# Eight output tiles of the last pass turned through DRAM and VectorE's block transpose, with POOL's products and the verdict moved

## The chip, the core and the metric

The kernel runs on one core of one Trainium2 chip. The metric is the time of one execution on the device in microseconds (us), the median of several runs. TensorE (PE) multiplies matrices and transposes through them, VectorE (DVE) and ScalarE (ACT) work element by element, POOL (GpSimd) does the same more slowly, and SP issues the transfers between DRAM and the on-chip memory. PSUM is the memory that TensorE writes to.

## The reference

Four layers on x of 2048 rows and 640 columns: a Fourier layer, a linear attention layer, and both again.

```python
x = A_x
x = x + _A_ref(_layernorm(x), A_dft_seq_re, A_dft_seq_im, A_dft_hid_re, A_dft_hid_im)
x = x + _B_ref(_layernorm(x), B_wqkv, B_wo)
...
# _A_ref: a = x @ hid_re.T, b = x @ hid_im.T;  y = seq_re @ a - seq_im @ b
# _B_ref: 32 heads of 20 columns; q, k, v = x @ wqkv; phi(t) = where(t > 0, t + 1, exp(t)) + 1e-6
#   kv = phi(k).T @ v per head;  z = sum of phi(k) over the rows
#   o = (phi(q) @ kv) / (phi(q) . z + 1e-6);  y = o @ wo
```

## The kernel before

The rows of x are cut into 16 tiles of 128 rows that stay on the chip. Every product of full precision is made of three products of rounded halves: a tile is split into `hi` (a ScalarE cast, L137) and `lo = src - hi` (a subtraction, L138, on VectorE or POOL), and `product` (L193) runs 5 chunks x 3 pairs x 2 column halves = 30 matmuls. Each product needs its tile with columns and rows exchanged. There are two ways to that. `transposed` (L143) does it on TensorE, five 128x128 transposes into PSUM, from which `hi` and `lo` are read. `turn_out` and `turn_in` (L151, L156) write the tile to DRAM in one order and read it back in another, both on the SP queue, and `turned` (L161) finishes with VectorE's transpose of 32x32 blocks; `hi` and `lo` are then read from that tile. Which tiles of the keys and queries stages go the second way stands in `TURNED`; in `TLOWS`, whose subtraction goes to POOL.

An attention layer first makes keys and queries of all tiles and the gram matrix (L286) in two parts (`keys_values`). `combine` then makes the key-value products (L465) and the matrix M that holds them and wo (six rows of products in `rows`), and does the last `KEEP` query projections of the layer (`late`).

The last pass is `outputs`: for tile n, POOL multiplies the query features with the sums of the keys (`weigh`, L511, "a product" of POOL below), and VectorE makes the weighted queries from it (`weighted`: a reduction L527, an addition L528, a reciprocal L529, and a pair of multiplications L531 and L537). The result is transposed on TensorE, split, and multiplied with M in 30 matmuls; VectorE adds the result to x (the residual, L611) and SP stores it. POOL works three tiles ahead, the weighting two, the transposes one. In the first round `between` calls `verdict`, which reduces the results of a check on the Fourier matrices to one flag (two small TensorE transposes, L1177 and L1181, and some small VectorE rows); the check itself compares 30 pieces of those matrices during the keys stages (`Check`, L1157, in the steps of `STEPS`).

Within a stage, TensorE, VectorE, ScalarE and POOL get their order from a scheduler at build time, which goes by program order, free buffers and the offsets in `AHEAD` ("weigh", "q", "res" and so on, by stage and tile). SP issues in program order. Temporary tiles come from a pool of 12 buffers (`temp`), weights and `slot` tiles from one of 31.

Of the kernel before, what the change touches and what calls it, by code (L numbers as in the profile page):

```python
# [15 lines left out]
NT = S // 128  # L16
# [14 lines left out]
STEPS = ((1, 2, 3, 4, 5, 6, 10, 11, 12), (2, 4, 8, 9, 12))  # L31
SAVES = ((4, 5, 8, 10, 13), (0, 6, 7, 11, 12))
# [4 lines left out]
TURNED = ((4, 5, 6, 7, 8, 9, 10, 11, 12, 13, 14, 15), (4, 5, 6, 8, 9, 10, 11, 12, 13, 14, 15))  # L37
TLOWS = ((3, 7, 15), ())
LEADS = (3, 2)
ORDERS = ('tfkq', 'tfkq')  # L40
ANORM = ((2,), (3, 5))
KEEP = (2, 1)
TOTAL = (4, 2)
EARLY = (14, 13)
PKSUMS = ((1, 7, 13, 14), (2, 6, 11, 12))
LEAD = 3
LOADS = (13, 13, 15, 15)
ASTATS = ((4, 10, 11, 13, 14), (1, 4, 10, 15))
VSTATS = ((0, 3, 4, 7, 8, 11, 13, 15), (1, 11, 13, 15))
# [8 lines left out]
class K:  # L58
# [77 lines left out]
    def split(self, src, hi, lo, pool=0):  # L136
        self.nc.scalar.copy(hi, src)  # L137
        self.engine(pool).tensor_tensor(lo, src, hi.bitcast(F32), op=ALU.subtract)  # L138
# [15 lines left out]
    def turn_in(self, src, early):  # L154
        z = self.pqp.tile([128, D], F32, tag="pq", name=self.nm("z")) if early else self.temp()
        self.nc.sync.dma_start(z, src.rearrange("a (j t) c -> (a j) (t c)", t=4))  # L156
        return z
# [40 lines left out]
class Attention:  # L198
# [99 lines left out]
    def keys_values(self, check=None, saves=()):  # L298
# [26 lines left out]
        for a, b in ((0, CUT), (CUT, NT)):  # L325
            pks = []
            for n in range(a, b):
                got, pk = [], self.slot()

                def feed(n=n):  # L330
                    for m in range(n + 1, n + 1 + lead) if n == 0 else (n + 1, n + lead):
                        if m < NT and m not in out and (m == n + 1 or m in self.turns):
                            with k.ahead("normed", m):
                                out[m] = self.normed(m)
                    for m in range(n + 1, n + 1 + fetch) if n == 0 else (n + fetch,):
                        if m < NT and m in self.turns:
                            out[m] = k.turn_in(out[m], m < EARLY[k.layer])

# [97 lines left out]
    def combine(self, G, late):  # L436
# [17 lines left out]
        with k.ahead("weigh", 0):  # L454
            qd, t1 = self.weighted(0, self.weigh(0)), self.weigh(1)
# [4 lines left out]
        for js in ((NE - 1, NE - 2), range(NE - 2)):  # L460
            kvps = k.psum()
            for j in js:
                e, w = span(j)
                for c in range(ND):
                    nc.tensor.matmul(  # L465
                        place(kvps, j), wv[c][:, e : e + w], G[c][:, e : e + w],
                        start=c == 0 and j in (5, 4, 0), stop=c == ND - 1 and j > 2, skip_group_check=True,
                    )
            for j in js:
                w = span(j)[1]  # L470
                km = place(kvps, j) if KM[k.part // 2] else k.temp(shape=(w, w))
                t = self.wt()
                hi, lo = t[:w, :w], t[:w, 128 : 128 + w]
                with k.ahead("kv", j):
                    nc.vector.tensor_tensor(km, place(kvps, j), self.mask[:w, :w], op=ALU.mult)
                    if w == EC:
                        k.split(km, hi, lo)
                    else:
                        k.split(km.rearrange("p (h i s) -> p h i s", i=ND, h=2), mixed(hi), mixed(lo))
                kv[j] = hi, lo  # L480
        for q in late[1:]:
            q()
# [22 lines left out]
        self.next, self.t1 = qd, self.weigh(2)  # L505

    def weigh(self, n):
        k = self.k
# [945 lines left out]
```

## Time and profile before

| what | us |
|---|---|
| three timed runs | 757.91, 758.84, 759.44 |
| their median | 758.84 |
| the profiled execution | 759.65 |
| its span, first to last instruction | 757.7 |
| TensorE busy | 732.2 (97%) |
| VectorE busy | 597.0 (79%) |
| ScalarE busy | 356.0 (47%) |
| POOL busy | 245.2 (32%) |

The span is what the rows of the profile cover; about 2 us lie around it. The profiled execution took 0.8 us more than the median run. A busy TensorE is a TensorE with work in it, not one at its peak.

### The profile page before, as it was taken

The numbers are of one execution on the slowest core, as the hardware profiler recorded it, in microseconds if no ns is written. First come the engines' busy times: TensorE is split into PE (matmuls) and PEld (weight loads), VectorE is DVE, ScalarE is ACT, GpSimd is POOL, SyncE is SP. The second block draws the span as 40 slices with busy tenths as digits, with TensorE's granted clock in tenths as the row PEclk, the third lists the DMA queues.
The fourth block names the chain that finished last, engine by engine and source line by source line (L and its number), as shares of the span: only waits on it lengthen the run. The fifth ranks groups of instructions, "written<-read, shape, count | busy, mean of one in ns | idle before, by whom it ended". The sixth has DMA issues, their size and how long they took to land.

```text
span 757.7 us, 12763 instructions
## 1 busy us (share of the span) xinstructions
PE 732.2 (97%) x4769; PEld 695.1 (92%) x4769; DVE 597.0 (79%) x1162; ACT 356.0 (47%) x673; POOL 245.2 (32%) x262
## 2 busy tenths in 40 slices
PE   4999999999999999999999999999999999989997
PEld 1388999999999999899976999999999999989997
DVE  7997888778769757788974867888776887598982
ACT  7745544574345524555682246556433555331110
POOL 5337932320013202467762664214000011233300
PEclk9999999999999999999999999999999999999999
DMA  9323247754576820400052223764236525011112
GB/s 333 99 82 100 81 145 253 240 179 126 163 219 209 292 68 23 128 30 2 10 194 75 70 93 96 233 203 145 75 111 186 177 69 164 2 29 53 70 71 74
DMA packets 50560, 94.22 MB, mean 124 GB/s; under 512 B 5013, under 2 KB 18584, under 8 KB 50488
## 3 DMA queue, kind: packets, MB, share of 16 engines
q1 hardware_dynamic: 50487, 93.31, 38.7%
q8 instruction: 40, 0.66, 0.4%
q14 instruction: 33, 0.26, 0.1%
HBM read 73.54 MB, written 19.33 MB: 123 GB/s over the span
## 4 chain that ended last, share of the span: by engine, by line
PE 71%; DVE 13%; DMA 5%; ACT 4%; POOL 2%; issue 2%; SPq 1%; DVEq 0%; ACTq 0%
PE ps L193 41%; PE ps L286 18%; PE ps L1028 4%; PE ps L1082 3%; DMA z<-turn 3%; PE ps L143 2%; PE ps L465 2%; DVE t L138 2%; PE ps L987 1%; DMA ck<-in_ck 1%; DVE t L531 1%; DVE ps L527 1%; DMA x<-in_x 1%; DVE x L553 1%; DVE junk L1157 1%
## 5 line engine op out<-in xcount | busy, mean ns | idle before, releaser
L193 PE MATMUL ps<-w,t 128*128 128x320 f32 x2880 | 435.7, 311 | 0.7 <-DVE w L138 0.3
L193 PEld LDWEIGHTS ps<-w,t 128*128 128x128 f32 x2880 | 424.2, 188 | 2.6 <-DVE t L138 0.6
L286 PE MATMUL ps<-t,t 128*128 128x256 f32 (+1 forms) x640 | 140.0, 309 | 0.2 <-ACT t L137 0.2
L1157 DVE CUSTOM_DVE_ANT_0 junk<-ck,ck 128x688 bf16<-128x688 f32 (+5 forms) x138 | 103.8, 752 | 7.9 <-DMA ck<-in_ck 6.2
L286 PEld LDWEIGHTS ps<-t,t 128*128 128x128 f32 x640 | 107.2, 188 | 0.4 <-ACT t L137 0.4
L353 POOL TENSOR_TENSOR t<-t,s 128x640 f32<-128x640 f32 x24 | 43.4, 1808 | 181.7 <-DVE s L321 174.7
L286 PE MATMUL ps<-w,t 128*128 128x384 f32 (+1 forms) x320 | 98.8, 310 | 2.6 <-DVE w L138 2.6
L318 ACT ACTIVATE t<-ps 128x640 f32<-128x640 f32 x64 | 45.1, 705 | 106.5 <-PE ps L193 106.1
L511 POOL TENSOR_TENSOR t<-pq,t 128x640 f32<-128x640 f32 x32 | 53.3, 1672 | 100.9 <-ACT t L434 45.9
L137 ACT CAST t<-t 128x640 fp32r<-128x640 f32 x55 | 40.0, 728 | 66.6 <-DVE t L161 28.0
L137 ACT CAST t<-ps 128x640 fp32r<-128x640 f32 (+1 forms) x43 | 29.6, 692 | 81.5 <-PE ps L143 80.9
L286 PEld LDWEIGHTS ps<-w,t 128*128 128x128 f32 x320 | 60.1, 188 | 3.7 <-DVE w L138 3.7
L138 DVE TENSOR_TENSOR t<-t,t 128x640 fp32r<-128x640 f32 x53 | 45.9, 865 | 20.7 <-ACT t L137 19.5
L1028 PE MATMUL ps<-t,u 128*128 128x322 f32 x306 | 48.7, 316 | 1.1 <-DVE t L138 0.7
L1028 PEld LDWEIGHTS ps<-t,u 128*128 128x128 f32 x306 | 46.0, 189 | 2.8 <-issue 1.0
L320 ACT ACTIVATE t<-t 128x640 f32<-128x640 f32 x64 | 47.4, 742 | 0.0
L138 DVE TENSOR_TENSOR t<-ps,t 128x640 fp32r<-128x640 f32 (+1 forms) x43 | 35.0, 816 | 8.7 <-ACT t L137 8.7
L321 DVE SCALAR_TENSOR_TENSOR pq<-t,pq 128x640 f32<-128x640 f32 x32 | 28.2, 881 | 14.3 <-ACT t L320 14.3
L112 POOL TENSOR_TENSOR kept<-ve,mhalf 128x1 f32<-128x1 f32 x32 | 21.1, 675 | 54.3 <-DVE ve L111 53.7
L1082 PE MATMUL ps<-cw,ab 128*128 128x512 f32 x80 | 35.4, 595 | 1.6 <-ACT t L812 1.0
L321 DVE SCALAR_TENSOR_TENSOR s<-t,s 128x640 f32<-128x640 f32 x32 | 26.6, 832 | 9.9 <-ACT t L320 9.9
L1082 PEld LDWEIGHTS ps<-cw,ab 128*128 128x128 f32 x80 | 14.8, 190 | 21.0 <-issue 18.6
(187 smaller groups left out, 951.4 us busy)
## 6 DMA issues: line engine op xcount, KB each, us to landing
ck<-in_ck SPq DMA_DIRECT2D x48, 346.0 KB
ck<-in_ck SPq DMA_DIRECT2D x48, 344.0 KB
turn<-t SPq DMA_DIRECT2D x23, 320.0 KB
save<-w SPq DMA_DIRECT2D x20, 320.0 KB
w<-save SPq DMA_DIRECT2D x20, 320.0 KB
z<-turn SPq DMA_DIRECT2D x18, 320.0 KB
x<-in_x SPq DMA_DIRECT2D x16, 320.0 KB
out<-x SPq DMA_DIRECT2D x15, 320.0 KB
```

Of the source, the lines that this page charges most:

```text
L137: self.nc.scalar.copy(hi, src)
L138: self.engine(pool).tensor_tensor(lo, src, hi.bitcast(F32), op=ALU.subtract)
L193: nc.tensor.matmul(pu[:m, 512 * h : 512 * h + HD], s, w[:, HD * h : HD * h + HD], start=first, stop=last)
L286: nc.tensor.matmul(self.place(G, c, part), x[:, 128 * c : 128 * c + 128], p[:, f : f + n], start=start and i == 0, stop=stop and i == 2, s ...
L318: nc.scalar.activation(h2(e), halves(pu), AF.Relu, scale=-1.0)
L320: nc.scalar.activation(e, e, AF.Exp, scale=-1.0)
L321: nc.vector.scalar_tensor_tensor(out, e, 1e-6, out, op0=ALU.add, op1=ALU.add)
L353: k.engine(n not in PKSUMS[k.layer]).tensor_tensor(pksum, pksum, pk, op=ALU.add)
L511: k.nc.gpsimd.tensor_tensor(t1, self.PQ[self.order2[n]], self.zb, op=ALU.mult)
L1028: self.k.nc.tensor.matmul(po[:, o : o + 322], s[:, f : f + 128], w[:, x, :], start=start, stop=stop)
L1082: self.k.nc.tensor.matmul(self.sum(j), T.out["o", q][:, 128 * j : 128 * j + 128], self.C[2, g], start=n == 0, stop=n == 3)
L1157: i = nc.vector.tensor_tensor_reduce(k.junk[:, : a.shape[1]], b, a, 1.0, 0.0, op0, op1, o)
```

## The change

In the second layer's `outputs`, the tiles of `QTURNS` (7 and 9 to 15) go through DRAM: their weighted queries are made `QLEAD` = 2 tiles earlier than the others', a ScalarE copy brings the columns into the order that the block transpose wants, and `turn_out`, `turn_in` and `turned` take the place of `transposed`. For tiles 10, 13 and 15 (`QLOWS`) the subtraction goes to POOL. POOL's products are made four tiles ahead (`WLEAD`), six for turned tiles, and nine of them (`WSLOTS`) lie in slots of the larger pool. The verdict is made in three steps in rounds 6, 7 and 8. The residuals of tiles 0 to 5 are stored in halves. `LULLS` is (0, 0), so nothing waits for a lull.

```diff
-KEEP = (2, 1)
+QTURNS = (7, 9, 10, 11, 12, 13, 14, 15)
+QLEAD = 2
+LULLS = (0, 0)
+WLEAD = 4
+WSLOTS = (6, 7, 8, 9, 11, 12, 13, 14, 15)
+VERDICT = 6
+QLOWS = (6, 10, 13, 15)
+HALVES = (0, 1, 2, 3, 4, 5)
+KEEP = (2, 2)
...
-    def outputs(self, after, between=lambda: None):
+    def outputs(self, after, between=lambda n: None):
...
-        wt, t1 = self.next, self.t1
+        wt, t1 = {1: self.next}, self.t1
+        turns, lead = (QTURNS, WLEAD) if self.saved else ((), 3)
+        early = lambda m: QLEAD if m in turns else 0
         for n, i in enumerate(self.order2):
-            nxt = self.weigh(n + 3) if n + 3 < NT else None
-            if n + 1 < NT:
-                tp = k.transposed(wt)
-            if n + 2 < NT:
-                with k.ahead("weigh", n + 2):
-                    wt = self.weighted(n + 2, t1)
-            t1 = nxt
+            for m in range(n + 3, n + 1 + lead + QLEAD):
+                if m < NT and m not in t1 and m not in wt and m - lead - early(m) <= n:
+                    t1[m] = self.weigh(m, self.slot() if m in WSLOTS else None)
+            if n + 1 < NT and n + 1 not in turns:
+                tp = k.transposed(wt[n + 1])
+            for m in range(n + 2, n + 3 + QLEAD):
+                if m in t1 and m - 2 - early(m) <= n:
+                    with k.ahead("weigh", m):
+                        wt[m] = self.weighted(m, t1.pop(m))
+                    if m in turns:
+                        mixed = self.slot()
+                        k.nc.scalar.copy(
+                            mixed.rearrange("p (a b i) -> p b a i", a=4, b=ND),
+                            wt[m].rearrange("p (b a i) -> p b a i", a=4, b=ND),
+                        )
+                        wt[m] = k.turn_in(k.turn_out(mixed), self.slot())
...
-            between()
+            between(n)
             if n + 1 < NT:
                 with k.ahead("q", n):
-                    q = k.split_chunks(tp)
+                    q = k.turned(wt[n + 1], n + 1 in QLOWS) if n + 1 in turns else k.split_chunks(tp)
...
-                after(i, hs[0], hs[-1] + 1)
+                for h in [(x, x + 1) for x in hs] if n in HALVES and self.saved else [(hs[0], hs[-1] + 1)]:
+                    after(i, *h)
...
-            att.outputs(store, lambda: flags or flags.append(verdict(k)))
+            steps = verdict(k)
+            att.outputs(store, lambda n: 0 <= n - VERDICT < 3 and flags.append(next(steps)))
```

With `KEEP` the second layer's last two query projections stand in `combine`, not one. Beside this the tables of the two keys stages are new. The first layer turns tile 2 as well (`TURNED`); `TLOWS`, `ANORM`, `ASTATS`, `VSTATS` and `PKSUMS` give other tiles' subtractions, normalisations, statistics and key sums to other engines: over both keys stages VectorE has seven normalisations, two sets of statistics and seven subtractions fewer and three key sums more. `TOTAL`, `EARLY`, `STEPS`, `SAVES` and some 60 entries of `AHEAD` change. With the new `STEPS` one of the 30 pieces of the check (the fifth of `in_ck3`) is fetched and not compared.

The order shows three places. First POOL, its products of the last pass. Before, one after the other by tile, all in temporary tiles `t`; a row is one product, and `pq` is a tile's query features.

```order
L511 TENSOR_TENSOR t_7571<-pq_6510,t_7225 128x640
L511 TENSOR_TENSOR t_7623<-pq_6902,t_7225 128x640
L511 TENSOR_TENSOR t_7675<-pq_7296,t_7225 128x640
L511 TENSOR_TENSOR t_7727<-pq_6621,t_7225 128x640
L511 TENSOR_TENSOR t_7779<-pq_4967,t_7225 128x640
```

Now, for tiles 4, 7, 6, 9, 5, 10, 8, 11, 12, 13 and 14 in this order (L532 is the same line), and then the first subtraction that goes to POOL (L146), of tile 10:

```order
L532 TENSOR_TENSOR t_7500<-pq_6523,t_7196 128x640
L532 TENSOR_TENSOR s_7555<-pq_6629,t_7196 128x640
L532 TENSOR_TENSOR s_7608<-pq_7366,t_7196 128x640
L532 TENSOR_TENSOR s_7661<-pq_5404,t_7196 128x640
L532 TENSOR_TENSOR t_7553<-pq_7267,t_7196 128x640
L532 TENSOR_TENSOR t_7729<-pq_5511,t_7196 128x640
L532 TENSOR_TENSOR s_7727<-pq_4966,t_7196 128x640
L532 TENSOR_TENSOR s_7782<-pq_5083,t_7196 128x640
L532 TENSOR_TENSOR s_7841<-pq_5212,t_7196 128x640
L532 TENSOR_TENSOR s_7917<-pq_5635,t_7196 128x640
L532 TENSOR_TENSOR s_7979<-pq_5742,t_7196 128x640
L146 TENSOR_TENSOR t_8091<-t_8089,t_8090 128x640
```

The products of tiles 6 to 9 and 11 to 14 now lie in slots (`s`), those of 8 and 11 to 14 directly behind each other.

Second VectorE, from the residual of tile 4 to that of tile 5 (`x_104`, `x_106`). Before:

```order
L611 TENSOR_TENSOR x_104<-x_104,ps_7742 128x640
L138 TENSOR_TENSOR t_7826<-ps_7781,t_7825 128x640
L527 TENSOR_REDUCE den_7891<-t_7831 128x32
L528 TENSOR_SCALAR den_7891<-den_7891 128x32
L529 RECIPROCAL rden_7892<-den_7891 128x32
L531 TENSOR_TENSOR t_7831<-pq_5417,rden_7892 128x5x120
L537 TENSOR_TENSOR t_7831<-pq_5417,rden_7892 128x2x5x4
L611 TENSOR_TENSOR x_106<-x_106,ps_7794 128x640
```

Now, from the subtraction of tile 6 to the block transpose of tile 9 (L146 was L138, L175 L161, L549 to L558 L528 to L537, L643 L611):

```order
L146 TENSOR_TENSOR t_7835<-ps_7784,t_7834 128x640
L175 STREAM_TRANSPOSE t_7909<-s_7687 128x4x160
L549 TENSOR_SCALAR den_7925<-den_7925 128x32
L643 TENSOR_TENSOR x_106<-x_106,ps_7803 128x640
L550 RECIPROCAL rden_7926<-den_7925 128x32
L552 TENSOR_TENSOR s_7782<-pq_5083,rden_7926 128x5x120
L558 TENSOR_TENSOR s_7782<-pq_5083,rden_7926 128x2x5x4
L146 TENSOR_TENSOR t_7911<-t_7909,t_7910 128x640
L548 TENSOR_REDUCE den_7981<-s_7841 128x32
L146 TENSOR_TENSOR t_7974<-ps_7919,t_7973 128x640
L175 STREAM_TRANSPOSE t_8035<-s_7801 128x4x160
```

A tile's rows were one subtraction, one weighting and one residual; a turned tile's block transpose comes on top, two residuals ahead of its product, and the weightings run up to four tiles ahead.

Third SP, from the store of tile 4 on. Before it was one store a tile:

```order
L1256 DMA out<-x_104 128x640
L1256 DMA out<-x_106 128x640
L1256 DMA out<-x_108 128x640
L1256 DMA out<-x_110 128x640
L1256 DMA out<-x_112 128x640
```

Now, `turn` being the tile in DRAM:

```order
L1291 DMA out<-x_104 128x320 x2
L166 DMA turn_7799<-s_7797 128x4x160
L170 DMA s_7801<-turn_7799 128x640
L1291 DMA out<-x_106 128x320 x2
L166 DMA turn_7859<-s_7857 128x4x160
L170 DMA s_7861<-turn_7859 128x640
L1291 DMA out<-x_108 128x640
L166 DMA turn_7934<-s_7932 128x4x160
L170 DMA s_7936<-turn_7934 128x640
```

The way out and back of tile 9 stands behind the store of tile 4, that of tile 10 behind the store of tile 5, and so on to tile 15 behind that of tile 10.

## Rows read from the trace of the kernel before

**Rows 1.** Windows: length, busy PE, PEld, DVE, ACT, POOL; granted clock, DMA share, GB/s

```profile
107.00:175.00 68.00, 66.97 (x451) 65.90 (x449) 54.24 (x99) 39.53 (x66) 16.00 (x13) 1.00 0.67 218
466.00:652.00 186.00, 186.00 (x1273) 185.79 (x1272) 145.37 (x291) 90.86 (x148) 23.93 (x19) 1.00 0.47 144
```

**Rows 2.** Waits of TensorE: us in total, times, longest

```profile
PE ps L705 <- DMA x<-in_x: 10.6, 1, 10.6
PE ps L286 <- DVE w L138: 2.6, 3, 1.1
PE ps L143 <- DVE t L537: 2.2, 1, 2.2
```

**Rows 3.** Chain that ended last, last pass: start us, us, what

```profile
675.33 1.46 DVE t L537
...
676.92 1.05 PE ps L143 x5
677.98 5.62 PE ps L193 x30
683.60 0.55 PE ps L143 x5
684.15 4.41 PE ps L193 x30
```

**Rows 4.** Windows of the last pass

```profile
677.00:680.00 3.00, 3.00 (x14) 3.00 (x15) 3.00 (x9) 0.69 (x1) 0.00 (x0) 0.53 0.04 14
680.00:683.60 3.60, 3.60 (x25) 3.59 (x24) 1.94 (x7) 0.00 (x0) 0.00 (x0) 0.92 0.21 84
...
688.00:719.00 31.00, 31.00 (x222) 30.95 (x221) 29.85 (x44) 4.26 (x7) 11.69 (x7) 1.00 0.17 65
719.00:743.50 24.50, 24.50 (x175) 24.47 (x175) 17.52 (x28) 3.38 (x5) 2.50 (x2) 1.00 0.18 69
```

**Rows 5.** Timeline of VectorE in the last pass: start us, us, instruction

```profile
685.82 0.81 DVE L138 TENSOR_TENSOR t<-ps,t 128x640 fp32r<-128x640 f32 x1
686.55 0.18 DVE L537 TENSOR_TENSOR t<-pq,rden 128x40 f32<-128x40 f32 x1
686.65 0.81 DVE L527 TENSOR_REDUCE den<-t 128x32 f32<-128x640 f32 x1
687.50 0.18 DVE L528 TENSOR_SCALAR den<-den 128x32 f32<-128x32 f32 x1
687.71 0.35 DVE L529 RECIPROCAL rden<-den 128x32 f32<-128x32 f32 x1
...
698.22 0.78 DVE L531 TENSOR_TENSOR t<-pq,rden 128x600 f32<-128x600 f32 x1
698.92 1.57 DVE L537 TENSOR_TENSOR t<-pq,rden 128x40 f32<-128x40 f32 x1
700.41 0.81 DVE L611 TENSOR_TENSOR x<-x,ps 128x640 f32<-128x640 f32 x1
```

**Rows 6.** Timeline of POOL in the last pass

```profile
688.69 1.58 POOL L511 TENSOR_TENSOR t<-pq,t 128x640 f32<-128x640 f32 x1 [3.45 <-issue]
...
718.36 1.57 POOL L511 TENSOR_TENSOR t<-pq,t 128x640 f32<-128x640 f32 x1 [3.40 <-PE ps L193]
```

**Rows 7.** Lines L161 and L138: duration ns min/median/max

```profile
L161 DVE STREAM_TRANSPOSE t<-z x18: 1319/1346/1370, 105.6 to 583.2; 128x640 f32<-128x640 f32 x18
...
L138 POOL TENSOR_TENSOR t<-t,t x2: 1571/1661/1751, 137.0 to 253.0; 128x640 fp32r<-128x640 f32 x2
```

**Rows 8.** Chain in the first layer's keys stage

```profile
111.61 0.38 SPq L151
...
115.99 1.35 DVE t L161
...
139.87 0.37 SPq L151
...
147.14 1.36 DVE t L161
```

More of the change, by code (lines that the diff above doesn't have):

```diff
@@ L137, in split, with behind @@
         self.nc.scalar.copy(hi, src)
-        self.engine(pool).tensor_tensor(lo, src, hi.bitcast(F32), op=ALU.subtract)
+        return self.engine(pool).tensor_tensor(lo, src, hi.bitcast(F32), op=ALU.subtract)
+    def behind(self, later, earlier):
+        if earlier is not None:
+            self.tc.add_manual_dep(
+                later.ins, earlier.ins.name, mybir.DependencyInfo(mybir.DependencyClass.Sync, mybir.DependencyReason.DATA),
+                reason="a lull",
+            )
     def transposed(self, src):
@@ L152, in turn_out, with turn_in @@
         return src
-    def turn_in(self, src, early):
-        z = self.pqp.tile([128, D], F32, tag="pq", name=self.nm("z")) if early else self.temp()
+    def turn_in(self, src, z):
         self.nc.sync.dma_start(z, src.rearrange("a (j t) c -> (a j) (t c)", t=4))
@@ L336, in feed @@
                         if m < NT and m in self.turns:
-                            out[m] = k.turn_in(out[m], m < EARLY[k.layer])
+                            early = m < EARLY[k.layer]
+                            z = k.pqp.tile([128, D], F32, tag="pq", name=k.nm("z")) if early else k.temp()
+                            out[m] = k.turn_in(out[m], z)
                 def turn(n=n):
@@ L454, in combine @@
         with k.ahead("weigh", 0):
-            qd, t1 = self.weighted(0, self.weigh(0)), self.weigh(1)
+            qd = self.weighted(0, self.weigh(0))
+            t1 = None if LULLS[k.layer] else self.weigh(1)
         late[0]()
@@ L476, in combine @@
                     if w == EC:
-                        k.split(km, hi, lo)
+                        lull = k.split(km, hi, lo)
                     else:
-                        k.split(km.rearrange("p (h i s) -> p h i s", i=ND, h=2), mixed(hi), mixed(lo))
+                        lull = k.split(km.rearrange("p (h i s) -> p h i s", i=ND, h=2), mixed(hi), mixed(lo))
                 kv[j] = hi, lo
+        if LULLS[k.layer]:
+            t1 = self.weigh(1, None, lull)
+        else:
+            lull = None
         for q in late[1:]:
@@ L504, in combine, with weigh @@
             self.M.append(m)
-        self.next, self.t1 = qd, self.weigh(2)
-    def weigh(self, n):
+        self.next, self.t1 = qd, {m: self.weigh(m, None, lull) for m in range(2, WLEAD if self.saved else 3)}
+    def weigh(self, n, t1=None, lull=None):
         k = self.k
-        t1 = k.temp()
+        t1 = k.temp() if t1 is None else t1
         with k.ahead("pz", n):
-            k.nc.gpsimd.tensor_tensor(t1, self.PQ[self.order2[n]], self.zb, op=ALU.mult)
+            k.behind(k.nc.gpsimd.tensor_tensor(t1, self.PQ[self.order2[n]], self.zb, op=ALU.mult), lull)
         return t1
@@ L547, in outputs_by_hand @@
         k, nc, X = self.k, self.k.nc, self.X
-        q, wt, t1 = self.first, {1: self.next}, {2: self.t1}
+        q, wt, t1 = self.first, {1: self.next}, self.t1
         pu = None
@@ L1175, in verdict @@
     nc.vector.tensor_tensor(both[:, 0:4], both[:, 0:4], low, op=ALU.max)
+    yield
     p = k.psum()
@@ L1179, in verdict @@
     nc.vector.tensor_reduce(top, p[:8, :128], axis=AX.X, op=ALU.max)
+    yield
     p = k.psum()
@@ L1189, in verdict @@
     nc.vector.tensor_copy(flag, bad)
-    return flag
+    yield flag
 def fast_path(k, ctx, x, wqkv, wo, mask, sign, cls, cex, hid, ckc, ckh, out):
```

25 lines of the change are left out of this document (13 added, 12 removed).

## The prediction

> **What bounds the kernel now.** I read three views: who waited for whom, the windows by stage, and the chain of the last pass. TensorE is the bound almost everywhere. In the stretch that covers the second layer's keys and queries it is busy for all of its 186 us, at a granted clock of 1.00 [rows 1]. Over the whole run three waits stand out: 10.6 us for the first load of x, 2.6 us in three pieces, none over 1.1 us, in the first layer's gram stage, and 2.2 us once in the last pass [rows 2]. So time can be won only by taking work off TensorE, or by removing one of these waits.
>
> The last pass (16 output tiles, a product of 30 matmuls for each) is a fixed beat: five transposes in 0.55 us, then 30 matmuls in 4.41 us, 4.96 us a tile [rows 3]. The reader should also see its bad start. After product 0, VectorE is in the second of the two multiplications that make tile 2's weighted queries (L537), which takes 1.46 us of the chain; TensorE waits 2.2 us [rows 2], and then its five transposes take 1.05 us and its 30 matmuls 5.62 us [rows 3]. The granted clock says why: it was 0.53 in the 3 us behind the gap, which is the lower of the two levels (1.2 and 2.4 GHz) for nearly all of that stretch, 0.92 in the next 3.6 us, and 1.00 later [rows 4].
>
> VectorE is the second bound. In 688 to 719 us it is busy 29.85 of 31.0 us; in 719 to 743.5 us, where POOL has only two products left, 17.52 of 24.5 us [rows 4]. The timeline shows the difference: the small multiplication L537 takes 0.18 us when POOL is quiet and 1.57 us when a POOL product (L511) started just before it [rows 5, 6]. One product thus costs VectorE about 1.4 us when the two meet. Reductions, residuals and subtractions from PSUM keep their 0.81 us, also beside a product.
>
> **The change, part by part.** (1) Eight tiles lose their TensorE transposes: 8 x 0.55 = 4.4 us off a stage that TensorE bounds [rows 3]. In their place VectorE gets eight block transposes of 1.35 us, which no POOL work ever stretched (1319 to 1370 ns over 18) [rows 7], together 10.8 us; ScalarE gets eight copies, and as it is busy 4.26 us in 31.0 [rows 4], even 2 us each would be hidden; three subtractions go to POOL at 1.66 us [rows 7], some 2.4 us off VectorE, and their tiles are transposed over 4 us before the product that needs them; the SP queue gets eight pairs of transfers. The trip from the issue of the way out to the block transpose is 4.4 us (111.61 to 115.99) and once 7.3 us (139.87 to 147.14) in the first layer [rows 8], where the core moved 218 GB/s [rows 1]. The last pass moves 65 to 70 GB/s [rows 4]; 640 KB more a tile of 4.41 us is 145 GB/s, together about the same 215, so I take these trips as they stand.
>
> (2) The start of the pass. The order puts the weighted queries of tile 2 right behind the last subtraction before product 0, ahead of residual 0; the verdict's two TensorE transposes and its small VectorE rows come six to eight tiles later; and one more query projection (30 matmuls) stands between the key-value products and the rows of M, which gives VectorE and POOL 4.41 us more before product 0. That projection is only moved, so TensorE's sum is the same. I count the whole loss at the start as gained: 2.2 us of waiting, 1.05 - 0.55 = 0.5 us in the transposes and 5.62 - 4.41 = 1.2 us in the product [rows 3], together 3.9 us. If VectorE is late here again the gain is nothing.
>
> (3) Does VectorE keep up? From the start of product 0 to the start of product 7 TensorE needs 7 x 4.41 + 5 x 0.55 = 33.6 us [rows 3]. The new order has these VectorE rows in that stretch: 8 reductions at 0.85 us from start to start, 9 additions at 0.21, 10 reciprocals at 0.35, 10 pairs at 0.70 + 0.10, 7 subtractions at 0.73 and 6 residuals at the same [rows 5], and one block transpose at 1.35 [rows 7]: 31.0 us, with some 0.5 us for the starts between them 31.5. That leaves 2.1 us. In the same stretch POOL has seven products to do (5, 10, 8, 11 to 14), and five of them no longer wait for a temporary buffer, so they run in a block. Bounds: none meets a pair, or all seven do, 7 x 1.4 = 9.8 us, a TensorE stall of 0 to 7.7 us. Following the queues row by row, product 10 should start when TensorE's product 1 has freed its buffer, 4.41 + 0.55 + 4.41 = 9.4 us in, and the block then lies on the pairs of tiles 5 and 6: four multiplications, of which the first finds POOL just done. I take three meetings, 4.2 us, less the 2.1: a stall of 2.1 us, in pieces of under 2 us around tiles 4 to 6. The clock fell behind a gap of 2.2 us; for these shorter ones I add nothing. Behind tile 7 VectorE has 2 us a tile to spare again.
>
> The Trainium skill (SBUF — State Buffer, "Who interferes with whom") speaks against this change: it says that a VectorE instruction with two SBUF inputs and a POOL instruction that reads SBUF lock each other out, the first to start holding the port for its whole length. The rows of L537 agree (1.57 us beside a product). By it a turned tile's subtraction, which now reads two SBUF tiles where it read one from PSUM, can be caught as well: seven products and three POOL subtractions, all caught, would cost 14 us, which is case B below at a higher price.
>
> (4) The rest. The first layer turns tile 2 as well, 0.55 us off TensorE. Over both keys stages VectorE has seven normalisations, two sets of statistics and seven subtractions fewer and three key sums more, and it compares 29 pieces instead of 30. In the second layer this cannot win anything, for TensorE is already full [rows 1]. In the first the 2.6 us of waits could go [rows 2], or others come; I take 0, with 1.5 us either way for a new order. The six early stores cut in halves are six more issues on SP, at 0.37 us the piece as for a way out [rows 8], in a pass of 80 us in which SP has a store a tile: nothing.
>
> Sum: -4.4 - 3.9 + 2.1 - 0.55 = -6.75 us. The profiled execution took 759.65 us, so 752.9; it lay 0.8 us above the median of the three timed runs, so the median should be 752.1 us.
>
> **Rivals.** A: VectorE keeps up entirely, because POOL's block falls on reductions and residuals. Then -8.85 us, 750.0. For it: the products of tiles 6 to 9 may be finished before product 0. Against it: all seven products from the one at 688.69 to the one at 718.36 [rows 6] met a pair.
> B: the gain is mostly eaten. All seven meet (+7.7 us) and a gap of over 2 us halves the clock once more (1.7 us as at the start): -8.85 + 9.4 = +0.55, 759.4, no change. For it: VectorE's 29.85 of 31.0 us [rows 4]. Against it: the pairs are only 8 of VectorE's 31.5 us in the stretch.
> C: the new order of the keys stages makes waits in the first layer, where the chain already runs through block transposes that wait for their loads [rows 8]. Two more waits like the longest of 1.1 us there [rows 2], and the rest of a stage's margin gone with them, cost about 3 us: 755.
> D, slower: the turned tiles form a loop through SP. The way out of tile m stands on SP behind the store of tile m-5, which waits for that residual; the block transpose of m stands on VectorE ahead of residual m-3. One round is store issue (0.4 us), trip, transpose 1.35, residual 0.73, and must fit into two tiles, 8.8 us; so the trip may take 6.3 us. At 10 us it sets 6.2 us a tile, 1.8 us more than 4.41, over eight tiles 14.6 us: -8.85 + 14.6, about 764.5. It decides from a trip of 8.5 us on (1.1 us a tile eats the 8.85). For it: the trip of 7.3 us, which would already set the beat, at 4.9 us a tile. Against it: that one was in flight with loads of the check, which the last pass has none of.
>
> **How the numbers follow.** Forecast 0.47 (751 to 754), A 0.22, C 0.13, B 0.11, D 0.07. About 0.2%, 1.5 us, is what a measurement of this kernel can tell from no change, so faster means under 757.3 and slower over 760.4: forecast, A and C are faster, 0.82; B is the same, 0.11; D is slower, 0.07. The range 748.7 to 757.4 holds the first three with the 1.5 us for the first layer; B and D are left out. The forecast's own range is 751 to 754.
>
> **What would show it.** In the last pass: no L143 rows from tile 9 on, 4.41 us a tile there; no wait of 2 us behind product 0 and a clock of 1.00 throughout; L531 or L537 rows of over 1.4 us three times between tiles 2 and 7, and TensorE waits for a VectorE subtraction that sum to about 2 us. SP trips under 6.3 us. A clock below 1.00 after tile 3 would speak for B, a TensorE wait for z loads for D. The prediction is wrong if VectorE stands still in this pass for a transfer, or if the first layer gains or loses more than 1.5 us.

## The result, and the profile after

The changed kernel takes 761.56 us (median of 20 runs, 758.36 to 764.91) where the kernel before took 759.19 us beside it: a ratio of 1.0030 (1.0018 to 1.0041), 0.3% slower. The prediction of 752.1 us, faster, was wrong, and the time lies outside its range.

Lines of the changed kernel: L207 is `product` (L193 before), L300 the gram matrix (L286), L158 TensorE's transposes (L143), L145 and L146 the cast and the subtraction of a split (L137, L138), L175 the block transpose (L161), L532 a POOL product (L511), L549, L552 and L558 the small steps and the pair (L528, L531, L537), L335 the feature map of keys and queries (L321), L1190 a comparison of the check (L1157), L482 the first key-value product (L465), L643 the residual (L611), L1291 the stores (L1256), L166 and L170 the way out and back (L151, L156).

Where the profiled spans differ, from the timelines of TensorE (us from the start of the span):

| | before | after | difference |
|---|---|---|---|
| key-value products, first layer | 292.10 | 295.34 | +3.2 |
| first gram product of the second layer | 531.68 | 535.22 | +3.5 |
| key-value products, second layer | 656.24 | 657.34 | +1.1, with one projection of 4.4 us fewer ahead of them: +5.5 |
| end of the last product | 752.33 | 753.59 | +1.3 |
| end of the span | 757.7 | 760.2 | +2.5 |

These are single executions; the first layer alone spreads by some 4 us over the profiles of kernels in which it is the same (288.8 to 293.0 us at its key-value products, in eight of them). By these two the first layer loses 3.2 us and the second layer's keys stage 2.0; from there to the last product the pass takes 96.25 us for 96.09 before, with the moved projection inside it, a gain of 4.2; and 1.2 us are lost behind the last product. TensorE's waits in the changed kernel (us in total, times, longest), to be held against [rows 2]:

```profile
PE ps L738 <- DMA x<-in_x: 10.3, 1, 10.3
PE ps L207 <- DVE t L146: 4.0, 4, 1.5
PE ps L207 <- ACT t L145: 3.0, 1, 3.0
PE ps L207 <- DVE den L549: 1.3, 1, 1.3
```

The waits for `w` at the gram matrix are down from 2.6 to 0.8 us, that of 2.2 us in the last pass is gone, and others stand in their place. The longest is new and lies in the first layer, where the kernel before had none. Windows of the changed kernel there (length, busy PE, PEld, DVE, ACT, POOL; granted clock, DMA share, GB/s):

```profile
249.00:252.00 3.00, 2.92 (x20) 2.65 (x19) 2.67 (x8) 0.58 (x1) 0.00 (x0) 1.00 0.54 134
252.00:255.00 3.00, 0.07 (x1) 0.07 (x1) 3.00 (x6) 0.85 (x2) 0.04 (x1) 0.85 0.82 189
255.00:258.00 3.00, 2.62 (x9) 2.22 (x10) 1.56 (x3) 2.95 (x5) 1.69 (x1) 0.50 0.98 329
258.00:261.00 3.00, 3.00 (x13) 3.00 (x13) 2.28 (x4) 0.00 (x0) 0.00 (x0) 0.51 0.68 267
261.00:264.00 3.00, 3.00 (x24) 3.00 (x23) 0.00 (x0) 1.25 (x3) 0.00 (x0) 1.00 0.44 125
```

TensorE stands still from 252 to 255 us, and behind the gap it runs at 0.50, the lower of its two levels (1.2 GHz): 22 matmuls in 6 us where the next 3 us have 24. The half clock alone costs some 3 us. By the mean clock of the runs it is not there in every execution: of the 20, the 15 with a mean clock of 0.995 or less have a median of 761.83 us, the three at 0.999 one of 759.40, which is still no gain on the kernel before.

The last pass itself did much of what was forecast. TensorE's timeline (start, us, instruction, idle time before it and what ended it):

```profile
673.03 2.90 PE L207 MATMUL ps<-w,w 120*120 120x320 f32 x18 [1.50 <-DVE t L146]
...
681.20 0.83 PE L207 MATMUL ps<-w,t 128*128 128x320 f32 x4 [0.42 <-DMA w<-t]
...
698.71 4.81 PE L207 MATMUL ps<-w,t 128*128 128x320 f32 x30 [1.27 <-DVE den L549]
...
722.34 31.25 PE L207 MATMUL ps<-w,t 128*128 128x320 f32 x210
```

At the end seven products run without a gap, 31.25 / 7 = 4.46 us each, where before one began every 4.96 us (the beat of [rows 3]). The start has waits of 1.5, 0.2 and 0.4 us at full clock in place of 2.2 us and the half clock [rows 3, 4]. The way through DRAM was longer than I had taken it. SP's timeline, and VectorE's, for the same tiles:

```profile
716.54 0.39 SPq L166 DMA_DIRECT2D turn<-s  x1
721.80 0.32 SPq L170 DMA_DIRECT2D s<-turn  x1
...
737.44 1.00 SPq L1291 DMA_DIRECT2D out<-x  x1
738.54 0.39 SPq L166 DMA_DIRECT2D turn<-s  x1
```

```profile
725.22 1.33 DVE L175 STREAM_TRANSPOSE t<-s 128x640 f32<-128x640 f32 x1 [1.09 <-DMA s<-turn]
...
730.38 1.34 DVE L175 STREAM_TRANSPOSE t<-s 128x640 f32<-128x640 f32 x1 [0.48 <-DMA s<-turn]
...
734.90 1.33 DVE L175 STREAM_TRANSPOSE t<-s 128x640 f32<-128x640 f32 x1 [0.70 <-DMA s<-turn]
736.08 0.81 DVE L643 TENSOR_TENSOR x<-x,ps 128x640 f32<-128x640 f32 x1
740.34 1.35 DVE L175 STREAM_TRANSPOSE t<-s 128x640 f32<-128x640 f32 x1 [3.46 <-DMA s<-turn]
...
745.25 1.34 DVE L175 STREAM_TRANSPOSE t<-s 128x640 f32<-128x640 f32 x1 [1.16 <-DMA s<-turn]
```

From the issue of the way out to the block transpose it is 8.7 us for the first of these tiles and 6.7 for the last (738.54 to 745.25); the six tiles from 711 us on lie between 6.4 and 8.7. VectorE waits for it, up to 3.5 us; TensorE, in this kernel, does not. The five block transposes above are those of tiles 11 to 15. They come 5.0 us apart ((745.25 - 725.22) / 4), slower than TensorE's 4.46, so the tiles' lead shrinks: tile 9 is transposed 8.3 us before its product starts, tile 15 only 3.9 us.

### The profile page after: what moved, and what is told of

Read it like the earlier page. It is cut to its first block, busy times and chain, and to the rows that moved or that the text cites. A ratio compares the mean times of both kernels' runs of the same rounds, so it can differ in the third digit from the quotient of the medians.

```text
span 760.2 us, 12712 instructions
## 1 busy us (share of the span) xinstructions
PE 729.3 (96%) x4724; PEld 691.2 (91%) x4724; DVE 586.2 (77%) x1144; ACT 371.4 (49%) x696; POOL 259.0 (34%) x276
## 4 chain that ended last, share of the span: by engine, by line
PE 65%; DVE 17%; DMA 6%; ACT 6%; POOL 3%; issue 3%; SPq 1%; DVEq 0%; ACTq 0%
PE ps L207 38%; PE ps L300 15%; DMA ck<-in_ck 4%; PE ps L1115 4%; PE ps L1061 4%; DVE junk L1190 3%; DVE t L146 2%; PE ps L482 2%; PE ps L1020 1%; DVE t L552 1%; DVE w L146 1%; DVE ps L548 1%; ACT t L844 1%; PE ps L158 1%; DVE x L574 1%
## 5 line engine op out<-in xcount | busy, mean ns | idle before, releaser
L207 PE MATMUL ps<-w,t 128*128 128x320 f32 x2880 | 436.5, 311 | 7.3 <-ACT t L145 3.0
L207 PEld LDWEIGHTS ps<-w,t 128*128 128x128 f32 x2880 | 424.9, 189 | 11.1 <-ACT t L145 4.9
L300 PE MATMUL ps<-t,t 128*128 128x256 f32 (+1 forms) x640 | 139.9, 309 | 0.0
L1190 DVE CUSTOM_DVE_ANT_0 junk<-ck,ck 128x692 bf16<-128x692 f32 (+6 forms) x133 | 102.0, 767 | 16.0 <-DMA ck<-in_ck 13.7
L300 PEld LDWEIGHTS ps<-t,t 128*128 128x128 f32 x640 | 107.0, 188 | 0.0
L300 PE MATMUL ps<-w,t 128*128 128x384 f32 (+1 forms) x320 | 98.4, 310 | 0.8 <-DVE w L146 0.8
L369 POOL TENSOR_TENSOR t<-t,s 128x640 f32<-128x640 f32 x21 | 38.1, 1813 | 159.8 <-DVE s L335 154.2
L145 ACT CAST t<-t 128x640 fp32r<-128x640 f32 x64 | 46.6, 728 | 89.9 <-DVE t L175 49.0
L532 POOL TENSOR_TENSOR t<-pq,t 128x640 f32<-128x640 f32 x23 | 36.6, 1602 | 77.1 <-ACT t L450 47.7
L146 DVE TENSOR_TENSOR t<-t,t 128x640 fp32r<-128x640 f32 x52 | 42.9, 825 | 24.1 <-PE ps L300 14.4
L300 PEld LDWEIGHTS ps<-w,t 128*128 128x128 f32 x320 | 60.2, 188 | 1.2 <-DVE w L146 1.1
L146 POOL TENSOR_TENSOR t<-t,t 128x640 fp32r<-128x640 f32 x12 | 19.9, 1660 | 78.7 <-ACT t L145 69.8
L335 DVE SCALAR_TENSOR_TENSOR s<-t,s 128x640 f32<-128x640 f32 x32 | 27.0, 843 | 21.2 <-ACT t L334 21.2
L145 ACT CAST t<-s 128x640 fp32r<-128x640 f32 x32 | 23.3, 729 | 37.8 <-DVE t L146 18.7
L335 DVE SCALAR_TENSOR_TENSOR pq<-t,pq 128x640 f32<-128x640 f32 x32 | 29.0, 907 | 14.9 <-ACT t L334 14.9
L145 ACT CAST t<-ps 128x640 fp32r<-128x640 f32 (+1 forms) x34 | 23.5, 690 | 32.2 <-PE ps L158 32.1
```

What stands on the lines that cost most here:

```text
L146: return self.engine(pool).tensor_tensor(lo, src, hi.bitcast(F32), op=ALU.subtract)
L207: nc.tensor.matmul(pu[:m, 512 * h : 512 * h + HD], s, w[:, HD * h : HD * h + HD], start=first, stop=last)
L300: nc.tensor.matmul(self.place(G, c, part), x[:, 128 * c : 128 * c + 128], p[:, f : f + n], start=start and i == 0, stop=stop and i == 2, s ...
L335: nc.vector.scalar_tensor_tensor(out, e, 1e-6, out, op0=ALU.add, op1=ALU.add)
L369: k.engine(n not in PKSUMS[k.layer]).tensor_tensor(pksum, pksum, pk, op=ALU.add)
L532: k.behind(k.nc.gpsimd.tensor_tensor(t1, self.PQ[self.order2[n]], self.zb, op=ALU.mult), lull)
```

## The experiments

All ratios are to the kernel before, run beside each kernel, with 95% intervals. 1.0% is 7.6 us. "Old" is what stood in the kernel before. The theory after the result: the new last pass gains, and the tables of the keys stages lose more. Rival: the last pass itself costs the time.

**1. The halves of the change.**

```diff
# last_only: the changed kernel with the old tables and priorities of the keys stages; KEEP stays (2, 2)
# keys_only: the kernel before with the new tables and priorities of the keys stages; KEEP stays (2, 1)
```

The kernels differ in 45 entries of `AHEAD`; the five that belong to the last pass stay new in last_only.

> The new last pass (eight tiles turned through DRAM, POOL's products, the verdict, the half stores, two kept queries) with every table of the two keys stages and every priority of the first three parts as before. Theory: the last pass gains 4.2 us up to the last matmul and gives back 1.2 us in its stores, the keys stages cost 5.5 us; so this runs in 759.2 - 3.0 = 756.2 us (755 to 757.5), and the first layer's end stands where it stood before (about 390 us at the second Fourier pass). Rival, the last pass itself costs the time and the later milestones of the first layer are only another placement: 760 us or more.

> The last pass and the count of kept queries of before, with the new tables of the keys stages (statistics, subtractions, sums, turned tiles, comparisons, saves, priorities). Theory: 759.2 + 5.5 = 764.7 us (763 to 766). Rival, the tables are neutral: 758.5 to 760 us.

last_only: 759.30 us, 1.0009 (0.9996 to 1.0021). keys_only: 760.89 us, 1.0025 (1.0010 to 1.0039). The tables do cost, 0.25% and not the 0.7% expected; but the new pass with two kept queries gains nothing, so the theory held only half.

**2. Which tables of the keys stages.**

```diff
# first_old: the changed kernel, first layer's entries and priorities old (not STEPS, SAVES)
# second_old: the same for the second layer's entries and priorities
# after_old_checks: STEPS and SAVES old; after_old_saves: SAVES old; after_old_steps: STEPS old
-STEPS = ((1, 3, 4, 5, 6, 10, 11, 12), (1, 4, 5, 7, 8, 9))
+STEPS = ((1, 2, 3, 4, 5, 6, 10, 11, 12), (2, 4, 8, 9, 12))
-SAVES = ((0, 2, 8, 13, 15), (2, 4, 5, 6, 8))
+SAVES = ((4, 5, 8, 10, 13), (0, 6, 7, 11, 12))
```

> The changed kernel with the first layer's entries of the turned tiles, subtractions, statistics, sums and priorities of before; comparisons, saves and the second layer's entries stay new. Theory: up to 3.5 us come back, 758.1 us, if the cause is in these entries; about 761.6 us if it is in the comparisons and saves, which stay as changed.

> The changed kernel with the second layer's entries of subtractions, statistics, sums and priorities of before; comparisons, saves and the first layer's entries stay new. Theory: the 2.0 us of the second layer's keys stage come back, 759.6 us. Rival, the second layer's entries are neutral or help: 761 us or more.

> The changed kernel with the places of the comparisons and of the weight stores (STEPS and SAVES) of before, all else as changed. Theory: the first layer's wait of 3.0 us near 253 us and the 6.8 us at half clock behind it (together about 6.4 us) come from these two tables; both go, the first layer ends at about 289 us instead of 295.3, and the time is 761.6 - 6.4 = 755.2 us (754 to 757). Rival, the cause is in the first layer's other entries (subtractions on POOL, turned tiles): the wait stays and the time is about 761.5 us. The run with those entries undone kept the wait, which speaks for the first.

> The changed kernel with only the places of the weight stores of before; the comparisons stay new. If the stores of the weights (two lie at tiles 13 and 15 now) crowd the transfers that the turned tiles need, the wait near 253 us goes and the time is about 755 us. If the places of the comparisons do it, it stays: about 761.5 us.

> The changed kernel with only the places of the comparisons of before; the weight stores stay new. The other half of the pair: about 755 us if the comparisons do it, about 761.5 us if the weight stores do. Were both needed for the wait, both of these runs would come out near 755 us.

first_old: 762.97 us, 1.0049 (1.0030 to 1.0068). second_old: 762.91 us, 1.0047 (1.0028 to 1.0067). Neither gave anything back, against my theory for both; both lie above the changed kernel's 1.0030, with intervals that overlap its own. In both, the wait near 255 us (2.4 us) and the half clock behind it stayed; keys_only had them too (1.8 us), last_only not. What these share is the places of the comparisons and stores, and this the next three show: after_old_checks 758.40 us, 1.0003 (0.9994 to 1.0012); after_old_saves 760.12 us, 1.0037 (1.0020 to 1.0053); after_old_steps 757.54 us, 1.0000 (0.9990 to 1.0010). The comparisons (STEPS) make the whole loss against the kernel before, 0.3% or 2.3 us; the stores none, as two pairs of runs show (with and without the old stores: 1.0003 and 1.0000, 1.0037 and 1.0030). The one profile of after_old_saves has a wait of 0.9 us there and no half clock; it is the fastest of its eight executions, and in three of the eight the mean clock is 0.995 or less, so that verdict rests on the runs. The profiled executions had led me to expect 6.4 us.

How they do it: groups of VectorE from 175 to 300 us, first in the changed kernel, then in after_old_steps (busy us, mean ns | idle before it, and what ended it).

```profile
L1190 DVE CUSTOM_DVE_ANT_0 junk<-ck,ck 128x688 bf16<-128x688 f32 (+5 forms) x39 | 29.6, 760 | 8.9 <-DMA ck<-in_ck 8.6
```

```profile
L1190 DVE CUSTOM_DVE_ANT_0 junk<-ck,ck 128x688 bf16<-128x688 f32 (+2 forms) x40 | 31.5, 787 | 2.4 <-DMA ck<-in_ck 1.9
```

Six groups of comparisons are placed in the first gram part now, where four were; their loads come late there (8.9 us of waiting), and the block transposes stand behind them on VectorE. The tile that TensorE needs at 252 us is transposed at 252.8. Over all twenty profiles this waiting separates the two tables: 4.8 to 8.9 us in the six kernels with the new `STEPS`, 0.9 to 2.6 us in the fourteen with the old. That it is the loads which make the transposes late is read from these rows; no run moved the loads alone. (The new places also leave one fetched piece of 30 without a comparison; the old ones compare all.)

**3. The second kept query.**

```diff
# last_only_keep1 = last_only, after_keep1 = the changed kernel, each with
-KEEP = (2, 2)
+KEEP = (2, 1)
# before_keep2 = the kernel before with KEEP = (2, 2)
```

> The new last pass on the old keys stages as before, but with one query of the second layer kept back instead of two. Theory: the second kept query takes one projection out of the keys stage, where the stage then waits 1.4 us more, and covers the start of the last pass; so here the keys stage ends at 656.2 us as before, the start of the pass waits some 2 us more than with two, and the time is 759 to 761 us. Rival, the second kept query earns nothing: 757.5 to 758.5 us.

> The changed kernel with one number changed: one query of the second layer kept back instead of two. Theory: the second kept query costs 4.6 us (1.4 in the keys stage, 2.6 in the last pass, the rest a spread) as between the two runs with the old keys stages; so 761.6 - 4.6 = 757 us. Rival, the second layer's new tables were drawn up for two kept queries and lose as much with one: 760 to 763 us.

> The kernel before with one number changed: two queries of the second layer kept back instead of one. Theory: the second kept query costs in the keys stage (1.4 us) and delays VectorE at the start of the pass whatever the pass is: 760.5 to 763 us. Rival, in the old pass it covers the wait of 2.2 us and the half clock at the start: 756 to 758 us.

last_only_keep1: 753.33 us, 0.9944 (0.9930 to 0.9959), faster than anything either theory had. after_keep1: 761.07 us, 1.0034 (1.0019 to 1.0048). before_keep2: 759.36 us, 1.0009 (0.9997 to 1.0022), no difference. So with the old tables the second kept query takes back all that the new pass gains, 0.65%, and with the new ones, and the new comparisons, it makes no difference; there the rival came true. before_keep2 lies between its theory and its rival. In last_only VectorE and TensorE show the price at the start of the pass:

```profile
666.04 2.06 DVE L335 SCALAR_TENSOR_TENSOR pq<-t,pq 128x640 f32<-128x640 f32 x1 [3.17 <-ACT t L334]
```

```profile
668.89 2.90 PE L207 MATMUL ps<-w,w 120*120 120x320 f32 x18 [1.45 <-DVE t L146]
```

The kept query's feature map stands on VectorE ahead of the splits for M; it waits 3.2 us for ScalarE and then takes 2.06 us instead of 0.82, beside a POOL product. The wait of 1.45 us that follows is not the whole price: of the 5.2 us between the two profiled spans, 1.4 lie in the keys stage, 2.6 in the pass, 0.6 behind the last product and 0.6 ahead of the second layer's gram products.

before_keep2 has the same wait in the old pass, and shows what it pays for:

```profile
668.80 2.90 PE L193 MATMUL ps<-w,w 120*120 120x320 f32 x18 [1.45 <-DVE t L138]
...
678.23 0.74 PE L143 MATMUL ps<-ident,t 128*128 128x128 f32 x5 [0.27 <-DVE t L537]
```

The wait of 2.2 us behind product 0 is down to 0.27 us and the half clock is gone. From the key-value products to the last product this pass takes 98.91 us, less the projection of 4.41 it is 1.6 us under the 96.09 of before; the keys stage gives 1.7 us back. So the projection does cover the start of the old pass, and the gain is spent in the keys stage.

With one kept query TensorE's timeline in last_only_keep1 is:

```profile
669.30 4.79 PE L207 MATMUL ps<-w,t 128*128 128x320 f32 x30 [0.35 <-DVE w L146]
...
691.84 4.05 PE L207 MATMUL ps<-w,t 128*128 128x320 f32 x26 [1.45 <-DVE t L146]
...
714.75 31.02 PE L207 MATMUL ps<-w,t 128*128 128x320 f32 x210
```

No wait behind product 0, no half clock, one stall of 1.45 us at product 4. From the key-value products (655.68) to the last product (745.77) it is 90.09 us against 96.09 before: the pass gains 6.0 us and gives 1.0 back behind the last product (6.3 us to the end of the span, 5.4 before). In the keys stage the projection that KEEP moves away had covered a wait: from the first gram product to the key-value products last_only takes 121.52 us, which is 1.4 more than the 124.56 us of before less the projection.

**4. Without the turned tiles.**

```diff
# no_turn_keep1 = last_only_keep1 with
-QTURNS = (7, 9, 10, 11, 12, 13, 14, 15)
-QLOWS = (6, 10, 13, 15)
+QTURNS = ()
+QLOWS = ()
```

> The new last pass with no tile turned (all sixteen by TensorE's transposes; POOL's products, the verdict and the half stores as changed), one kept query, old keys stages. Theory: eight turned tiles are worth 8 x 0.50 = 4.0 us and cost up to 1 us behind the last product, so this runs at 753.3 + 3 to 4 = 756.3 to 757.3 us, and the start of the pass has no half clock. Rival, the moves of POOL's products and of the verdict alone make the gain: 753 to 754 us.

759.70 us, 1.0020 (1.0007 to 1.0033): 0.76% above last_only_keep1, 5.8 us, more than the 4 us of eight transposes. The timelines of POOL, VectorE and TensorE show why it is more:

```profile
666.74 14.78 POOL L532 TENSOR_TENSOR s<-pq,t 128x640 f32<-128x640 f32 x9
```

```profile
673.33 1.73 DVE L552 TENSOR_TENSOR t<-pq,rden 128x600 f32<-128x600 f32 x1
674.98 1.52 DVE L558 TENSOR_TENSOR t<-pq,rden 128x40 f32<-128x40 f32 x1
```

```profile
676.65 1.18 PE L158 MATMUL ps<-ident,t 128*128 128x128 f32 x5 [2.43 <-DVE t L558]
```

Without the turned tiles' earlier places nine POOL products run in one block from 666.7 to 681.5 us, over tile 2's pair; the wait of before comes back at 2.43 us, with the half clock. The 4.0 us of the transposes and some 4 us at the start, less the stall of 1.45 us that this run does not have, make the difference of 6.9 us between the two passes (96.98 and 90.09 us). So the moves of POOL's products and of the verdict alone do not free the start; the gain at the start hangs on where POOL's blocks lie. The other half, turned tiles with POOL's products and the verdict where they were, was not run, so what each of them is worth by itself stays open.

**5. Why one kept query does not help with the new tables.** All start from the changed kernel with KEEP = (2, 1) and the old STEPS, or name their base.

```diff
# after_steps_keep1: these two edits alone
# best_of_both: and the second layer's tables and priorities old; best_last_split: and QLOWS = (6, 10, 13)
# lull_keep1: after_steps_keep1 and LULLS = (0, 1); old_pz_keep1: and '2pz0', '2pz1', '2zb' old
# old_prio_keep1: and all the second layer's priorities old
# old_tabs_keep1: and the second layer's tables old, e.g.
-TLOWS = (..., (1, 4, 9, 10))
+TLOWS = (..., ())
-ANORM = (..., (1, 3, 4, 5, 7, 8, 12, 14))
+ANORM = (..., (3, 5))
```

> The new last pass with one kept query, the first layer's new entries and weight stores, and the comparisons and the second layer's entries of before. Theory: the first layer's entries save 2.9 us (waits before the gram products 0.4, 0.2, 1.1 and 0.6, and one tile's transposes 0.55), the last pass about 5: 753.3 - 2.9 = 750.4 us. Rival, the entries of the first layer pay only with the new comparisons: 753 us or more.

> The changed kernel with the comparisons of before and one kept query; the second layer's entries stay new. It differs from best_of_both (753.6 us) by those entries alone and from after_old_steps (757.5 us) by one kept query alone. Theory: the three POOL products meet the four small subtractions at the start of the last pass, TensorE waits some 3 us and runs at half clock; 757 to 758.5 us. Rival, the meeting in the earlier run came from the late first layer: 753.5 to 754.5 us.

> As after_steps_keep1, and POOL's products for the second and later tiles of the last pass made to wait for the last of the small subtractions (LULLS of the second layer set). Theory of the meeting: the four subtractions take about 0.9 us instead of 5.6, no half clock at the start, and the time is 753.5 to 754.5 us. Rival, the meeting only moves to the next VectorE work (the splits of the combined weights): no gain on after_steps_keep1.

> As after_steps_keep1, with the three priorities of POOL's first products (2pz0, 2pz1, 2zb) of before. If these set the meeting: 753.5 to 754.5 us. If other entries of the second layer do (statistics, subtractions, sums): as after_steps_keep1, 757 to 758.5 us.

> As best_of_both, with the last tile's subtraction on VectorE instead of POOL. There TensorE waits 0.82 us at 741.4 us for POOL's 1.56 us subtraction; on VectorE it takes 0.82 us. Theory: that wait goes, 753.6 - 0.8 = 752.8 us. Rival, the end is set by the stores behind: 753.6 us.

> As after_steps_keep1 with all the second layer's priorities of before, its tables new. If the priorities set the order of POOL's products and VectorE's work at the start of the last pass: the four subtractions take 0.85 us, no half clock there, about 753.6 us. If the tables do: 5.6 us, a wait of 3.3 us, 759 to 761 us.

> As after_steps_keep1 with the second layer's tables of before, its priorities new: the other half. About 753.6 us if the tables set the meeting, 759 to 761 us if the priorities do.

| | us | ratio (interval) | the four subtractions, us |
|---|---|---|---|
| after_steps_keep1 | 760.61 | 1.0027 (1.0012 to 1.0042) | 5.65 |
| old_pz_keep1 | 759.11 | 1.0013 (1.0003 to 1.0024) | 5.63 |
| old_prio_keep1 | 757.72 | 0.9986 (0.9974 to 0.9999) | 4.29 |
| old_tabs_keep1 | 753.96 | 0.9945 (0.9928 to 0.9963) | 0.85 |
| best_of_both | 753.58 | 0.9934 (0.9916 to 0.9952) | 0.85 |
| best_last_split | 753.76 | 0.9936 (0.9916 to 0.9955) | 0.85 |
| lull_keep1 | 763.01 | 1.0054 (1.0035 to 1.0073) | 0.85 |

The second layer's tables weigh most: with the old ones alone the kernel is 0.8% faster than with the new. The priorities are not idle: old ones on the new tables give 0.4%, between the two values that I had set. best_of_both missed its 750.4 us: it is no faster than last_only_keep1, so the first layer's new entries earn nothing that these runs can tell. Nor do tables and kept queries add up one by one (comparisons old throughout; in the old row the first layer is old too, except best_of_both):

| second layer's tables | one kept query | two |
|---|---|---|
| old | 0.9944 (last_only_keep1), 0.9934 (best_of_both) | 1.0009 (last_only) |
| new | 1.0027 (after_steps_keep1) | 1.0000 (after_old_steps) |

With the old tables the second kept query costs 0.65%, with the new ones it earns 0.3%. In after_steps_keep1, VectorE, POOL and TensorE at the start of the last pass:

```profile
664.67 5.65 DVE L146 TENSOR_TENSOR w<-t,w 120x120 fp32r<-120x120 f32 x4
```

```profile
663.96 4.69 POOL L532 TENSOR_TENSOR t<-pq,t 128x640 f32<-128x640 f32 x3 [5.79 <-PE ps L482]
668.61 4.64 POOL L532 TENSOR_TENSOR s<-pq,t 128x640 f32<-128x640 f32 x3
```

```profile
671.10 4.43 PE L207 MATMUL ps<-w,w 120*120 120x320 f32 x18 [3.26 <-DVE t L146]
```

and the same in old_tabs_keep1:

```profile
661.25 0.85 DVE L146 TENSOR_TENSOR w<-t,w 120x120 fp32r<-120x120 f32 x4
```

```profile
659.75 1.54 POOL L532 TENSOR_TENSOR t<-pq,t 128x640 f32<-128x640 f32 x1 [5.85 <-PE ps L482]
662.00 3.11 POOL L532 TENSOR_TENSOR t<-pq,t 128x640 f32<-128x640 f32 x2 [0.71 <-PE ps L158]
```

Four subtractions of 0.2 us each, between the key-value products and M, take 5.65 us when POOL's products follow one another, and 0.85 us when they fall into a gap of 0.7 us between two of them. In after_steps_keep1 TensorE then waits 3.3 us for the split behind them, and the products of M that follow run at a granted clock of 0.69 and 0.63 in the next two stretches of 2.5 us (4.43 us for 18 matmuls, 2.90 in last_only's row above). The lull run takes the meeting away, the subtractions are at 0.85 us again, and yet it is slowest: POOL starts the products only at 666.2 us, and TensorE waits 6.51 us for a pair (L558) that needs one of them:

```profile
677.58 1.30 PE L158 MATMUL ps<-ident,t 128*128 128x128 f32 x5 [6.51 <-DVE t L558]
```

The meeting is thus shown by its rows and by the tables, not by that run. Nor does it account for the whole difference between after_steps_keep1 and old_tabs_keep1: of the 6.2 us between their profiled spans, 2.7 lie in the last pass (94.24 and 91.56 us), 0.7 in the keys stage, and 2.6 in the first layer, which has the same entries in both. best_last_split made its wait shorter (0.82 to 0.37 us) and gained nothing.

## Why the prediction was wrong

**The step that failed: "I take 0, with 1.5 us either way for a new order" (4).** I counted the instructions that the keys stages gained and lost and not the order that the tables give them. The comparisons' new places alone cost 2.3 us (after_old_steps), which is rival C's mechanism in the first layer, with a half clock behind its wait that C did not price. I had also taken it that the second layer cannot win anything; it could lose: its keys stage took 2.0 us more in the profile. Of these, 1.4 are there with the old tables too (last_only) and go with the second kept query; some 0.6 are left for the tables.

**The second failed step: the moved projection "gives VectorE and POOL 4.41 us more before product 0" (2).** It also gives VectorE the kept query's own feature map ahead of the splits that TensorE waits for, and takes a cover from the keys stage. In the old pass it did cover the start, as I had it (before_keep2); in the new one the start is free without it (last_only_keep1), and only the price is left. By last_only and last_only_keep1 the second kept query costs 0.65%, 4.9 us, with the old tables: "I count the whole loss at the start as gained" held with one kept query and not with two. I wrote that without the gain VectorE would be late again; that was so, through a row I had not listed.

**The sum of the pass.** -4.4 - 3.9 + 2.1 = -6.2 us was forecast for the last pass; last_only_keep1 shows -6.0, and the changed kernel -4.2. That -6.0 comes so close is in part luck: it belongs to one kept query, where two were forecast, and what (1) had too much and what (3) had too much nearly cancel. (1) is 8 x 0.50 = 4.0 us, as the beat falls by 0.50 and not 0.55. (3) forecast a stall of 2.1 us around tiles 4 to 6 from POOL's block of five products; it is 1.27 us at product 4 (1.45 in last_only_keep1). VectorE in the changed kernel, beside POOL's block from 686.76 to 697.05:

```profile
687.30 1.08 DVE L549 TENSOR_SCALAR den<-den 128x32 f32<-128x32 f32 x1
...
689.03 0.88 DVE L549 TENSOR_SCALAR den<-den 128x32 f32<-128x32 f32 x1
...
691.95 1.55 DVE L558 TENSOR_TENSOR t<-pq,rden 128x40 f32<-128x40 f32 x1
...
694.16 1.46 DVE L552 TENSOR_TENSOR s<-pq,rden 128x600 f32<-128x600 f32 x1
695.54 1.56 DVE L558 TENSOR_TENSOR s<-pq,rden 128x40 f32<-128x40 f32 x1
```

The block starts 10.1 us after product 0 (9.4 forecast) and three rows of pairs take over 1.4 us, as told. The mechanism was right, the size was not: TensorE does six transposes between the starts of products 0 and 7, not five, which leaves it 0.55 us more, and the additions (L549) met the block too, which the sum did not have. A and B fall with it: there is one stall, and no second half clock in the pass.

**D and the trip.** The 4.4 and 7.3 us [rows 8] were misread: those block transposes belong to an earlier tile's way out than the one beside them, for the keys stage fetches each tile back one round later. The trip is 6.4 to 8.7 us, over the 6.3 that I had set as the most the loop allows, and TensorE's beat still is 4.46. D's loop is there all the same, with VectorE standing still for a transfer, which I had named as a sign of being wrong. One round of it, from the transpose of tile 13 (734.90) over the residual (736.08), the store (737.44) and the way out (738.54) to the transpose of tile 15 (745.25), takes 10.35 us for two tiles. What D had wrong is that it charged this to TensorE from the first tile on: with eight turned tiles the lead is not used up. It is in old_tabs_keep1 and best_of_both, where the last product waits 1.1 and 0.8 us for tile 15's subtraction. A cost of the turned tiles may also lie behind the last product: from there to the end of the span the kernels with them take 5.9 to 7.3 us, those without 5.4 to 5.9. The late residuals push the last stores together (from 748 to 752 us the core moves 252 GB/s, 123 before), but whether that makes the difference was not tested.

**What stays open.** Why the tables put POOL's products one way or the other (the wait for a transposition, L158, in the last row above suggests a buffer) was narrowed to the second layer's tables, with a share for its priorities, and no further. Open too is what the first layer adds to the differences between kernels in which it is the same.

## What to carry to other kernels

Where a change carries new scheduling tables along, run it with the old tables before judging the idea: here the idea was worth 0.6%, and what came with it (tables, the comparisons' places, a second kept query) cost 0.9%. Try such companions together as well as one by one: here a table that was bad with one kept query was good with two. Price a meeting of VectorE and POOL by the number of VectorE instructions that fall beside a run of POOL's, above all where TensorE waits for a string of small ones. And work that is moved to cover a wait brings its own element-wise work along; see where that lands.

## What was not expected of the hardware

A 120x120 subtraction of 0.2 us took up to 1.66 us beside back-to-back POOL products of 1.55 us, so four of them cost as much as 7 large instructions. It is not the pairs alone that POOL's products stretch: the feature map went from 0.82 to 2.06 us, and a step on 32 columns with a single input (L549) from 0.16 to 1.0 us in last_only at 673.15. The Trainium skill (SBUF — State Buffer, "Who interferes with whom") says that whichever of the two engines issues first holds the shared port for its whole instruction, and that a `tensor_scalar` with one input can be caught as well, in a mode that uses both ports; the rows agree with both (1.66 us beside products of 1.55 us, and 1.0 us for L549), though none shows in which mode L549 ran.
